# A fused attention and MLP block: a shorter hold in the planned order of the K/V stage, and another order of the first attention tiles

## The chip, the core and the metric

One core of a Trainium2 chip runs the whole block in one launch. The metric is the device time of that launch in microseconds (us), the median over several executions. A second source is one execution taken by the hardware profiler, in which every instruction has a start and a duration. The engines: PE (TensorE, matrix products), DVE (VectorE), ACT (ScalarE), POOL (GpSimd), and SP, whose queue issues nearly all DMAs. Each engine executes its own instructions strictly in the order in which the program lists them; semaphores make one wait for another.

## The reference

```python
def reference(A_x, A_wqkv, A_wo, B_x, B_W_gate, B_W_up, B_W_down):
    x = A_x                                     # (1, 2048, 1024) bf16
    h = x + attention(layernorm(x), A_wqkv, A_wo)
    return h + glu(layernorm(h), B_W_gate, B_W_up, B_W_down)

# attention: 32 heads of 32; phi(t) = where(t > 0, t + 1, exp(t)) + 1e-6
#   q, k, v = split(x @ wqkv);  pq, pk = phi(q), phi(k)
#   kv = pk^T v and z = sum(pk) per head, over all 2048 tokens
#   o = (pq kv) / (pq z + 1e-6);  result o @ wo
# glu: (relu(x @ W_gate) * (x @ W_up)) @ W_down      with 3584 columns
```

This is linear attention: kv and z need all tokens before the first o can be formed.

## The kernel before

**Tiling.** The 2048 tokens are 16 tiles of 128. The big products (K, V, Q, gate, up, down) are done as 2 x 2 block products with seven partial products in place of eight. One such block product is a `Quad` (lines 326 to 368). It works in three PSUM banks, A, D and E: p1 writes A (and ACT's `fork`, line 729, copies A to D), p6 adds into A, of which ACT's `snap` (line 732) takes a copy in SBUF, p5 writes E, p7 adds into A, a second snap follows, p2 adds into D, and after it the results c22 (E plus the second snap) and c11 (D) are read; p4 adds into A (c21), p3 adds into E (c12, with the first snap). So p4 has to wait for the second snap, and p3 for the read of c22. `Quads.run` (line 388) puts p4 and p3 of the previous quad between p1 and p6 of the next. Each p of 4 matmuls of 128x512 lasts some 0.86 us.

The two halves of the 2 x 2 scheme on the token side are tiles t and t + 8, which form pair t. The products need sums of the two halves' transposed, normalised tokens: `left_sums` (line 621) makes four of them on DVE: S1 = a21 + a22, S2 = S1 - a11, S4 = a12 - S2, S3 = a11 - a21. The weights' differences (`WForms.sums`, line 596, and `GW.sums`, line 971) are made on DVE as well.

**Stages.** In this trace: an opening, in which pair 0 runs as plain products; the K/V stage, a K quad and a V quad for each of the pairs 1 to 7, with the accumulation of kv (`kv_acc`, line 809) in banks 5 to 7, to about 122 us; the Q stage for the two blocks s = 0 and s = 1 of 512 columns each; the attention tiles of block 0 (`Tile_`, line 1004), woven into the Q quads of block 1, between 145 and 197 us; the first gate and up products with the attention tiles of block 1 woven in; gate and up to some 566 us; the down products to the end.

**The norm chain of a tile in the K/V stage** (`Norm`, lines 644 to 708). The x tile is loaded (SP). For tiles of the first half (t < 8) DVE takes the statistics (`stat`, two instructions, and `aggr`); for tiles of the second half ACT does, with a copy that sums up and a square that sums up (lines 664 and 667), between which POOL forms the negated mean (`neg`). Two short ACT steps form 1/std (`rstd_`, lines 681 and 683), POOL normalises the tile (`finish`, line 699), and SP issues a transposing DMA (line 701) and the load of a tile two pairs on. After tile 15 the four loads of WQ's parts follow on SP (lines 703 to 707).

**phi** (`phi_quad`, line 743): of each K or Q result ACT takes exp, DVE a clamp (`phi_clamp`) and a join (`phi_join`); c12 and c22 are added on DVE first (line 756), and `exp2` and `join2` treat both together.

**An attention tile** (`Tile_`): `group` for three groups of heads (PE products with kvz into one of banks 5 to 7, two short ACT steps, one DVE multiplication), after which SP transposes o; `wo(0)` and `wo(1)` (8 matmuls each, then a residual add on DVE); `square` (store of h by SP, negated mean), `square2` (ACT), `norm` (two ACT steps, POOL's normalisation, SP's transpose into the buffer that the gate and up products read). A tile with i = 1 also starts `left_sums` some ticks later (lines 1084 to 1086): the one with tt = 1 for two tiles' columns, those with tt = 2 and 3 for one.

**What sets the order.** Nothing is issued directly. `Plan.take` (line 115) records each instruction as a node with its predecessors, an estimated length (`hold`) and latency; so in the profile all instructions stand at line 123. The program text only gives TensorE's nominal order, by which `order` (line 182) gives each node a latest due time (`late`). `schedule` (line 202) then plays the engines forward on its own estimated clock, in nanoseconds, and lists each engine's instructions. TensorE takes the ready node that is earliest in the nominal order, within a window. Every other engine takes, of the nodes that are ready, the one with the earliest due time; but if a node with a due time more than 1500 ns earlier will be ready within `wait`, the engine is left idle until then and takes that one. `wait` is a multiple of the length of the instruction that could run now:

```python
    SHORT = 215000.0                                       # line 43
    wait = (1.2 if s < self.SHORT else 0.5) * v.hold       # line 246
```

The orders that come out are fixed in the program; the chip's own times do not change them.

Of the kernel before, what the change touches and what calls it, by code (L numbers as in the profile page):

```python
# [32 lines left out]
class Plan:  # L33
# [6 lines left out]
    WINDOW = 6000.0  # L40
    AHEAD = 120000.0
    OPENING = 45000.0
    SHORT = 215000.0

    class Node:
        __slots__ = ("eng", "calls", "preds", "hold", "lat", "open", "dma", "late", "ready", "left", "start", "nom")
# [155 lines left out]
    def schedule(self):  # L202
        nodes = self.nodes
        succs = self.order()
        engines = ("tensor", "vector", "scalar", "gpsimd", "sync")
        avail = {e: [] for e in engines}
        clock = {e: 0.0 for e in engines}
        for i, v in enumerate(nodes):
            v.left, v.ready = len(v.preds), max(0.0, v.late - self.AHEAD) if v.dma else 0.0
            if v.eng != "tensor" and v.late > 2.0 * self.OPENING:  # L210

                v.ready = max(v.ready, self.OPENING)
            if not v.left:
                avail[v.eng].append(i)
        pe = [i for i, v in enumerate(nodes) if v.eng == "tensor"]
        done, first, wire, out = set(), 0, 0.0, []
        while True:
            best = None
            for e in engines:
                a = avail[e]  # L220
                if not a:
                    continue
                if e == "sync":
                    for i in a:
                        v = nodes[i]
                        if v.late - max(clock[e], v.ready) > 6000.0:
                            v.ready = max(v.ready, wire - 2000.0)
                if e == "tensor":
                    while first < len(pe) and pe[first] in done:
                        first += 1  # L230
                    limit = nodes[pe[first]].nom + self.WINDOW
                    a = [i for i in a if nodes[i].nom <= limit]
                    if not a:
                        continue
                s = max(clock[e], min(nodes[i].ready for i in a))
                if best is None or s < best[0]:
                    best = (s, e, a)
            if best is None:
                break
            s, e, a = best  # L240
            now = [i for i in a if nodes[i].ready <= s]
            i = min(now, key=lambda i: (nodes[i].nom if e == "tensor" else nodes[i].late, i))
            v = nodes[i]
            if e != "tensor":

                wait = (1.2 if s < self.SHORT else 0.5) * v.hold
                soon = [j for j in a if s < nodes[j].ready < s + wait and nodes[j].late < v.late - 1500.0]
                if soon:
                    i = min(soon, key=lambda j: (nodes[j].late, j))
                    v = nodes[i]  # L250
                    s = v.ready
            v.start = s
            clock[e] = s + v.hold
            end = s + v.hold + v.lat
            if v.dma:
                wire = max(wire, s + v.hold) + v.dma
                end = wire + v.lat - v.dma + min(4000.0, max(0.0, 0.25 * (v.late - s)))
            elif e == "sync":

                end = max(end, min(wire + 800.0, end + 2500.0))  # L260
            avail[e].remove(i)
            done.add(i)
            out.append(i)
            for j in succs[i]:
                w = nodes[j]
                r = clock[e] if w.eng == e else end
                w.ready = max(w.ready, r)
                w.left -= 1
                if not w.left:
                    avail[w.eng].append(j)  # L270
        assert len(out) == len(nodes)
        self.span = max(clock.values())
        return out
# [205 lines left out]
def block_kernel(ctx: ExitStack, tc: tile.TileContext, x, wqkv, wo, wg, wu, wd, out, H: int):  # L479
    nc = tc.nc  # L480
    P = 128
# [12 lines left out]
    SW = 512  # L494
    NS = 2
# [296 lines left out]
    def v_quad(p):  # L792
        v = v_ring()

        def blk(i, j):
            return v[:, i, j * KH:(j + 1) * KH, 0:P]

        def copy(i, j):
            return lambda ps: nc.scalar.copy(out=blk(i, j), in_=split(ps))

        def add(i, j):
            return lambda ps, u: nc.vector.tensor_tensor(out=blk(i, j), in0=split(ps), in1=split(u), op=ALU.add)

        return v, Quad(tok_prod(p, WV), fork, snap,
                       {"c11": copy(0, 0), "c12": add(0, 1), "c21": copy(1, 0), "c22": add(1, 1)}, five_banks)
# [106 lines left out]
    for p in range(1, NP):  # L912
# [6 lines left out]
        v, vq = v_quad(p)  # L919
# [166 lines left out]
                return (lag_s[0], chain_of(*left_sums(self.s * SW + (self.tt + 1 - n) * P, n * P)))  # L1086

    lag_s, turned = [3], []
    tiles = [Tile_(s, i, tt) for s in range(NS) for tt in range(SW // P) for i in range(2)]

    def w(m, j):
        return lambda: tiles[m].wo(j)
# [440 lines left out]
@with_exitstack  # L1533
def kernel(
    ctx: ExitStack,
    tc: tile.TileContext,
    A_x: bass.AP,
    A_wqkv: bass.AP,
    A_wo: bass.AP,
    B_x: bass.AP,  # L1540
    B_W_gate: bass.AP,
    B_W_up: bass.AP,
    B_W_down: bass.AP,
    out: bass.AP,
):
    block_kernel(tc, A_x, A_wqkv, A_wo, B_W_gate, B_W_up, B_W_down, out, H=32)
# [30 lines left out]
```

## Time and profile before

| what | us |
|---|---|
| median of 4 executions | 726.79 (726.66 to 727.04) |
| the profiled execution, its time | 726.7 |
| its span, first to last instruction | 724.9 |
| TensorE not busy within the span | 13.7 |
| ACT busy, DVE busy in 90 to 110 us | 9.7 and 12.3 of 20 |
| ACT busy, DVE busy in 30 to 50 us | 14.6 and 16.8 of 20 |
| ACT busy, DVE busy in 200 to 210 us | 6.9 and 9.6 of 10 |

The page of a profile gives for each engine the busy time, its share of the span and the number of instructions; then the span in 40 slices, a digit each, in tenths of the slice. A timeline lists instructions in order of time, equal ones that follow each other in one line: start, us from that start to the end of the last, engine, line, operation, output and input with partitions x elements and type, count, and in brackets the idle time of the engine just before, with the engine or DMA whose signal ended it. An instruction's duration holds some 0.1 us of its end that overlaps the next on the same engine. Times in the text are us from the start of the span.

### The profile page before, as it was taken

What the parts mean: (1) busy time and instruction counts of PE and PEld (TensorE: products, weight loads), DVE (VectorE), ACT (ScalarE), POOL (GpSimd) and SP (SyncE); (2) the same over time, 40 slices, a digit from 0 to 9 for tenths busy, and PEclk for the clock granted to TensorE, in tenths of its full rate; (3) what the DMA queues carried; (4) which work ended last, traced back from release to release, by engine and by line L of the source; (5) the groups of instructions that cost most, each with busy time, mean ns of one, the idle gap of its engine ahead of it and who ended that gap; (6) DMA issues with size and microseconds to landing.
All of it is one profiled execution on the core that took longest, in us unless ns stands there. A gap on an engine that the chain in (4) does not pass through costs nothing.

```text
span 724.9 us, 11180 instructions
## 1 busy us (share of the span) xinstructions
PE 711.2 (98%) x4112; PEld 396.9 (55%) x4163; DVE 566.4 (78%) x954; ACT 277.1 (38%) x540; POOL 81.8 (11%) x88
## 2 busy tenths in 40 slices
PE   8998999999999999999999999999999999999998
PEld 3444545444444444444444444444444688888887
DVE  6887765788897965566766968769858879899996
ACT  5787644666655343333333333333333220001100
POOL 1343100002201220000000000000000004001452
PEclk9999999999999999999999999999999999999999
DMA  9544805249855540446145584685681878777974
GB/s 287 149 89 101 200 4 183 52 92 212 199 123 146 131 102 1 128 142 182 59 145 181 169 252 144 199 262 184 201 262 51 275 261 213 213 267 234 248 78 60
DMA packets 156503, 117.40 MB, mean 162 GB/s; under 512 B 54944, under 2 KB 140192, under 8 KB 156320
## 3 DMA queue, kind: packets, MB, share of 16 engines
q1 hardware_dynamic: 148832, 113.01, 54.0%
q0 software_dynamic: 7616, 3.67, 4.8%
q8 instruction: 32, 0.52, 0.3%
q14 instruction: 23, 0.19, 0.1%
HBM read 70.52 MB, written 34.08 MB: 144 GB/s over the span
## 4 chain that ended last, share of the span: by engine, by line
PE 88%; ACT 2%; DVE 1%; issue 1%; DMA 0%; POOL 0%; ACTq 0%; DVEq 0%
PE psum L123 88%; ACT mem L123 1%; DVE mem L123 1%; DMA mem<-mem 0%; ACT tiny L123 0%; ACT psum L123 0%; DVE tiny L123 0%; POOL tiny L123 0%; ACTq L123 0%; DVEq L123 0%
## 5 line engine op out<-in xcount | busy, mean ns | idle before, releaser
L123 PE MATMUL psum<-mem 128*128 128x512 bf16 (+4 forms) x4096 | 710.3, 334 | 10.2 <-ACT mem L123 2.5
L123 PEld LDWEIGHTS <-mem 128*128 128x128 f16 (+1 forms) x4163 | 396.9, 98 | 324.2 <-issue 11.0
L123 DVE TENSOR_TENSOR mem<-psum,mem 128x512 f32<-128x512 f32 (+2 forms) x240 | 187.3, 794 | 102.1 <-ACT mem L123 70.8
L123 DVE TENSOR_TENSOR mem<-mem 128x512 f16<-128x512 bf16 (+8 forms) x400 | 244.1, 650 | 8.2 <-DMA mem<-mem 2.9
L123 ACT COPY mem<-psum 128x512 f32<-128x512 f32 (+2 forms) x124 | 92.7, 749 | 215.3 <-PE psum L123 211.1
L123 ACT COPY psum<-psum 128x512 f32<-128x512 f32 (+1 forms) x68 | 49.1, 722 | 158.3 <-PE psum L123 156.1
L123 POOL DMA_DIRECT2D out_dram<-mem x28 | 34.1, 1299 | 412.1 <-DVE mem L123 412.0
L123 POOL TENSOR_SCALAR mem<-mem,tiny 128x1024 bf16<-128x1024 bf16 x28 | 40.7, 1455 | 181.4 <-ACT tiny L123 168.9
L123 ACT ACTIVATE mem<-psum 128x512 bf16<-128x512 f32 x90 | 53.7, 597 | 18.9 <-PE psum L123 18.2
L123 DVE SCALAR_TENSOR_TENSOR mem<-mem 128x512 bf16<-128x512 bf16 (+1 forms) x71 | 57.3, 807 | 1.2
L123 DVE SCALAR_TENSOR_TENSOR mem<-psum,mem 128x512 bf16<-128x512 f32 x66 | 45.2, 687 | 12.5 <-PE psum L123 10.2
L123 DVE TENSOR_SCALAR mem<-mem 128x512 bf16<-128x512 bf16 (+1 forms) x49 | 17.3, 354 | 19.9 <-ACT mem L123 19.1
L123 ACT ACTIVATE mem<-mem,tiny 128x1024 bf16<-128x1024 bf16 x24 | 27.5, 1144 | 8.4 <-DVE tiny L123 5.9
L123 DVE TENSOR_TENSOR mem<-psum,tiny 128x384 bf16<-128x384 f32 (+1 forms) x48 | 22.8, 507 | 4.3 <-ACT tiny L123 3.9
L123 ACT ACTIVATE mem<-mem 128x1024 bf16<-128x1024 f32 (+1 forms) x23 | 24.3, 1056 | 2.9 <-DVE mem L123 2.7
L123 ACT ACTIVATE tiny<-tiny 128x1 f32<-128x1 f32 (+2 forms) x112 | 22.5, 206 | 6.5 <-DVE tiny L123 3.7
L123 ACT ACTIVATE tiny<-psum 128x12 f32<-128x12 f32 (+1 forms) x48 | 8.0, 170 | 17.5 <-PE psum L123 17.2
L123 DVE BATCH_NORM_STATS2 tiny<-mem 128x6 f32<-128x512 bf16 x16 | 10.3, 683 | 2.5 <-DMA mem<-in_A_x_dram 2.5
L123 ACT CAST mem<-psum 128x512 bf16<-128x512 f32 x18 | 10.6, 587 | 4.2 <-PE psum L123 3.7
L123 POOL TENSOR_SCALAR tiny<-tiny 128x1 f32<-128x1 f32 x14 | 5.3, 383 | 39.0 <-ACT mem L123 21.4
L123 ACT ACTIVATION_READ_ACCUMULATOR mem<-mem,tiny 128x1 f32 x24 | 4.5, 188 | 0.0
L123 DVE TENSOR_SCALAR tiny<-tiny 128x1 f32<-128x1 f32 x16 | 3.4, 210 | 0.4
(18 smaller groups left out, 14.4 us busy)
## 6 DMA issues: line engine op xcount, KB each, us to landing
l_dram<-mem SPq DMA_DIRECT2D x98, 128.0 KB, 2.3
mem<-l_dram SPq DMA_DIRECT2D x12, 896.0 KB, 6.3
mem<-in_A_x_dram SPq DMA_DIRECT2D x32, 256.0 KB, 3.0
mem<-in_B_W_up_dram SPq DMA_DIRECT2D x14, 512.0 KB, 5.4
mem<-in_B_W_gate_dram SPq DMA_DIRECT2D x14, 512.0 KB, 4.3
mem<-in_B_W_down_dram SPq DMA_DIRECT2D x28, 256.0 KB, 3.8
r_dram<-mem SPq DMA_DIRECT2D x56, 128.0 KB, 2.0
mem<-r_dram SPq DMA_DIRECT2D x8, 896.0 KB, 5.2
```

The costliest lines, as they stand in the source:

```text
L123: call = lambda: getattr(getattr(self.nc, eng), op)(*args, **k)
```

## The change

The planner's rule gets a lower bound: the long hold (1.2 of an instruction's length) now applies only between 120000 and 215000 ns of the planner's clock, and the short one (0.5) before and after. And the list of attention tiles of block 0 is ordered by half first: tt = 0 to 3 of half 0, then tt = 0 to 3 of half 1, where the halves alternated; block 1 keeps its order.

```diff
-    SHORT = 215000.0
+    MIXED = (120000.0, 215000.0)
...
-                wait = (1.2 if s < self.SHORT else 0.5) * v.hold
+                wait = (1.2 if self.MIXED[0] < s < self.MIXED[1] else 0.5) * v.hold
...
-    tiles = [Tile_(s, i, tt) for s in range(NS) for tt in range(SW // P) for i in range(2)]
+    tiles = [Tile_(0, i, tt) for i in range(2) for tt in range(SW // P)]
+    tiles += [Tile_(1, i, tt) for tt in range(SW // P) for i in range(2)]
```

Compared as lists, both programs hold the same instructions on each engine. The places at which the lists differ, given in the times that the instructions have in the trace of before: SP from 15 to 18 us (tile 2's load ahead of tile 9's transpose), 55 to 85 and 151 to 191; DVE from 17 to 111 and 150 to 227; ACT from 29 to 79 and 149 to 188; POOL from 34 to 189; PE from 149 to 184 (other tiles in the same places) and 209 to 212 (one p5 product of the gate quads ahead of a p3). Everywhere else they are the same.

In the K/V stage, for example, ACT's list around tile 13's square, from the snap at 52.57 us of the trace of before on, reads:

```
before: snap 1; square of tile 13; ln step of 13; exp of c11; exp step of 13; snap 2; fork
after:  square of tile 13; ln step of 13; snap 1; exp step of 13; exp of c11; ln and exp step of tile 6; snap 2; fork
```

## The prediction

> **What bounds the kernel now.** I read the page first (busy times, slices), then the waits of TensorE, then the timelines of TensorE, ScalarE, GpSimd and VectorE around its gaps.
>
> ```profile
> PE 711.2 (98%) x4112; PEld 396.9 (55%) x4163; DVE 566.4 (78%) x954; ACT 277.1 (38%) x540; POOL 81.8 (11%) x88
> PE   8998999999999999999999999999999999999998
> ...
> PEclk9999999999999999999999999999999999999999
> ```
>
> TensorE is busy for 711.2 of 724.9 us at full granted clock, and the change leaves its products as they are. Only the 13.7 us in which it is not busy can move. Of these, windows put 3.7 into the first 30 us, 2.5 into 30 to 70, some 1.9 into 149 to 210 and 3.5 behind 700, where no engine's order changes (the orders of both programs differ only between 15 and 227 us of this trace).
>
> ```profile
> 30.40 25.34 PE L123 MATMUL psum<-mem 128*128 128x512 bf16 x137 [1.42 <-DVE mem L123]
> 57.61 2.75 PE L123 MATMUL psum<-mem 128*128 128x512 f16 x12 [1.87 <-ACT mem L123]
> 152.20 19.52 PE L123 MATMUL psum<-mem 128*128 128x512 bf16 x110 [0.57 <-DMA mem<-mem]
> 172.06 4.95 PE L123 MATMUL psum<-mem 128*128 128x512 bf16 x27 [0.34 <-DVE mem L123]
> 177.35 2.87 PE L123 MATMUL psum<-mem 128*128 128x512 bf16 x14 [0.34 <-DVE mem L123]
> ```
>
> In brackets stands the idle time ahead of the piece. The two gaps that matter are in the K/V stage: 1.42 us (product p3 of pair 1's K quad waits until VectorE has read bank E) and 1.87 us (p4 of pair 3's K quad waits until ScalarE has snapshot bank A). How the second comes about:
>
> ```profile
> 50.50 4.33 POOL L123 TENSOR_SCALAR mem<-mem,tiny 128x1024 bf16<-128x1024 bf16 x2
> 54.80 0.20 POOL L123 TENSOR_SCALAR tiny<-tiny 128x1 f32<-128x1 f32 x1
> ...
> 52.57 0.57 ACT L123 COPY mem<-psum 128x512 f32<-128x512 f32 x1
> 55.04 1.15 ACT L123 ACTIVATE mem<-mem,tiny 128x1024 bf16<-128x1024 bf16 x1 [1.89 <-POOL tiny L123]
> ...
> 56.99 0.58 ACT L123 COPY mem<-psum 128x512 f32<-128x512 f32 x1
> ```
>
> GpSimd normalises tiles 12 and 5 (4.33 us), then forms tile 13's negated mean. ScalarE stands 1.89 us for that mean, squares tile 13 (1.15), and only then makes the snapshot (56.99) that TensorE waits for. The normalisation is not urgent; being late, it has come to lie in front of urgent work.
>
> **The change, part by part.** No instruction is added or removed, on any engine or queue; orders differ.
>
> *Shorter hold before 120 us of planner time.* An engine now waits at most 0.5, not 1.2, of an instruction's length for more urgent work. So in the K/V stage statistics, normalisation and sums move forward past snapshots, forks and phi work; nothing urgent moves forward past them. I followed the new queues by hand with this trace's durations; times below are of this trace, the new ones with a "now".
>
> First gap. VectorE before:
>
> ```profile
> 20.54 3.49 DVE L123 TENSOR_TENSOR mem<-mem 128x512 f16<-128x512 bf16 x5 [2.23 <-DMA mem<-mem]
> ...
> 24.89 4.66 DVE L123 TENSOR_TENSOR mem<-mem 128x2048 f16<-128x2048 bf16 x4
> 29.47 0.28 DVE L123 TENSOR_SCALAR mem<-mem 128x512 bf16<-128x512 bf16 x1
> 29.67 0.68 DVE L123 TENSOR_TENSOR mem<-psum,mem 128x512 f32<-128x512 f32 x1
> ```
>
> The 2.23 us of idleness at 18.3 (tile 9's transpose has to land) is now filled with one weight difference (1.13), a clamp (0.33) and a join (0.61), which leave the queue behind: -2.07. On SP, tile 2's load is now ahead of tile 9's transpose: +0.5. Two statistics of tile 3 (0.60 each) are now ahead of the add at 29.67: +1.2. Net -0.4; the gap goes from 1.42 to about 1.0. Bounds: -1.4 (gap gone), and +1.2 if the filling buys nothing.
>
> Second gap, all in shifted time (0.4 earlier). Tile 12's second 1/std step stood at 50.09, behind two snapshots, a cast and an exp (1.07); now it stands at 45.2, just behind its square and one snapshot. So tile 12's normalisation starts at 45.3, not 50.50; tile 5's follows at 47.8; tile 13's mean is there by 49.7 and its square, behind a cast that ends at 50.2, starts then and not at 55.04. The 1.89 us go. What is late next: the snapshot is now also behind tile 6's two 1/std steps, which wait for VectorE, which waits for tile 12's transpose. 45.3 + 2.5 (GpSimd, half of 4.33 taken upward) + 1.24 (issue) + 2.2 (landing: tile 10's issue ended at 32.00, the sum that needs it began at 34.22) = 51.2. Behind it three left sums (0.34 each), an add (0.60), a left sum, two statistics (1.2) and the aggregate (0.2): 54.6. Two 1/std steps (0.4) and the snapshot (0.58): 55.6. TensorE wants it at 55.37 - 0.4 = 55.0. So about 0.6 of the old gap (2.0 between matmul starts) stays: -1.4. Bounds: -2.0 and 0.
>
> Rest of the stage. I went through every product up to 118 us whose buffer is freed less than 1.6 us before it. The tightest are again adds on VectorE with left sums in front: tile 14's transpose must land first (now at 67.3; the add behind is wanted at 69.4), then tile 15's (now 72.7; wanted 76.5, with 2.4 us of work between: 1.3 to spare). A join that now precedes the c22 add (43, 58, 71, 97, 110 us) falls into idleness of 0.27 to 0.60 ahead of that add: nothing, at most 0.3 each. WQ's loads follow tile 15's transpose and start some 10 us sooner; their sums move with them, into VectorE's idle stretches (82.88: 2.24 us idle). Cost zero.
>
> *First halves' tiles first.* Tile slots on TensorE keep their places, only which tile fills them changes; per slot the same matmuls, three group normalisations, two residual adds, square, normalisation and transpose. Gaps of 0.57, 0.34 and 0.34 stand, since what makes them (the first transpose of o; a gate-weight difference of 1.07 in front of a residual add) stands at the same place. What moves: the left sums need both halves, so those of the first two blocks (four sums, 0.6 to 1.1 us) go from 180-186 to behind 190 us, where VectorE has less room: 8.09 of 10 us busy in 190 to 200, 9.60 in 200 to 210, all of 210 to 220. The new order puts the three S4 sums (0.60 + 2 x 0.34, some 1.3 us) last, at about 207.5 to 209.3, and one p5 product ahead of the p3 that needs them; p3 then starts at 209.7. Gate-weight differences give way (earliest use 221 us). I take 0; bounds -0.4 and +1.3 (all of the S4 work on the path).
>
> Sum: -0.4 - 1.4 + 0 = -1.8. The profiled execution took 726.7 (span 724.9 and 1.8 around it), the median is 726.79: forecast **724.9**.
>
> A rule that speaks against it: normalisations on GpSimd took 4.95 (25.79, two of them) and 4.33 us where an undisturbed one took 1.19 (57.25), and a weight difference 1.98 (27.49) where others took 1.13. The Trainium skill, SBUF — State Buffer, section "SBUF: two separate sides", calls the port pair of VectorE and GpSimd an exclusive lock: whoever comes second stands for the whole instruction, also against a VectorE operation with two SBUF inputs. By that rule each early normalisation can cost VectorE 1.19 us, and with one such on the chain the sum would be -0.6, 726.1; rows say only that it happens in some places (the add on the path reads PSUM and SBUF and kept its 0.67 to 0.69 everywhere).
>
> **Rivals.**
> *The waits only change their name* (0.24): the second gap stays whole, because tile 6's 1/std steps, now in front of the snapshot, come late. For it: the slowest two normalisations (2.5 each) put 12's landing 1.2 us later than the fastest, and everything behind it is one chain. Against: ScalarE's own queue gets to them 4 us sooner. 726.7 - 0.4 + 0 = 726.3. The attention's pile-up (+1.3, so 726.2) counts here too.
> *Left sums in front of the phi work* (slower, 0.17): VectorE is in order, and tile 15's left sum is now three places ahead of the add that frees bank E for p3 of pair 6's V quad. In this trace tile 15's transpose was issued at 80.97 and its sum ran at 84.94. Each us of landing after 74.0 costs TensorE a us. If the chain through SP, ScalarE and GpSimd advances by half of what I worked out (9.8 us, counted on TensorE's clock), it lands at 77.6: +3.6, 728.5. Against: tile 15's square stands, on ScalarE, ahead of work that is needed at 69 us.
> *It doesn't do what it says* (in the first's chance): the order is that of a plan, and the plan's clock is not the chip's.
>
> **How the numbers follow.** My forecast 0.59 (own range 723.8 to 726.0), unchanged name or pile-up 0.24, slower 0.17. A difference of 0.2% (1.45 us) is what a measurement tells from none: faster means below 725.3. Of my own case some 0.07 lie above that. Faster 0.52, same 0.31, slower 0.17. Range: downward -1.4 - 2.0 = -3.4 if both gaps vanish, 723.3; upward to 727.9, toward the slower rival until 2 in 10 are out.
>
> **What would show it.** Right: TensorE's gap ahead of pair 1's p3 near 1.0 us; ScalarE no longer standing for GpSimd before tile 13's square, which runs near 50 us; a gap of at most 0.8 us near 55; TensorE about 1.8 us ahead of its old times from 56 us to the end. Wrong: a gap by VectorE behind a DMA between 64 and 80 us; VectorE without a pause from 190 to 222 us with gaps of TensorE at 201 to 212; the 1.87 us unchanged under another releaser.

## The result, and the profile after

| | us | ratio to before (95%) |
|---|---|---|
| before, median of 52 executions | 726.75 | |
| changed, median of 34 executions | 725.84 (724.48 to 727.14) | 0.9988 (0.9983 to 0.9993) |
| changed, the profiled execution | 725.6, span 723.8 | |

The change gains 0.9 us: clear of noise, since the interval of the ratio ends below 1, but half of the 1.8 us of the forecast and less than the 0.2% (1.45 us) that the prediction calls a difference. The busy line of the page and TensorE's timeline of the changed kernel:

```profile
PE 711.7 (98%) x4112; PEld 396.6 (55%) x4163; DVE 564.5 (78%) x954; ACT 277.3 (38%) x540; POOL 78.6 (11%) x88
```

```profile
29.41 25.69 PE L123 MATMUL psum<-mem 128*128 128x512 bf16 x137 [0.50 <-DVE mem L123]
55.67 21.50 PE L123 MATMUL psum<-mem 128*128 128x512 f16 x118 [0.57 <-ACT mem L123]
77.44 2.75 PE L123 MATMUL psum<-mem 128*128 128x512 bf16 x12 [0.26 <-DVE mem L123]
...
151.06 19.54 PE L123 MATMUL psum<-mem 128*128 128x512 bf16 x110 [0.58 <-DMA mem<-mem]
170.95 4.94 PE L123 MATMUL psum<-mem 128*128 128x512 bf16 x27 [0.35 <-DVE mem L123]
176.25 30.61 PE L123 MATMUL psum<-mem 128*128 128x512 bf16 x149 [0.35 <-DVE mem L123]
```

The first gap fell from 1.42 to 0.50 us of idleness, the second from 1.87 to 0.57, under the same releasers. A piece that starts at 77.44 is new: TensorE waits there for VectorE. The three gaps of the attention stand as they stood (0.58, 0.35, 0.35).

For the account I take the start of the same product in two traces and write the difference (negative: sooner than before). The first 13 us differ from one execution to the next although the order of every engine is the same there, so a stage is read from the difference of two columns:

```
us in the trace of before   13     35     50     60     74     82    205    700
changed                  -0.07  -0.99  -0.64  -1.94  -1.58  -1.16  -1.09  -1.17
```

First gap -0.92, 35 to 50 us +0.35, second gap -1.30, 60 to 74 us +0.36, 74 to 82 us +0.42, attention +0.07, the rest of the program -0.08. From 13 us on that is -1.10. How the second gap came down, from ScalarE's and GpSimd's timelines of the changed kernel:

```profile
50.44 1.15 ACT L123 ACTIVATE mem<-mem,tiny 128x1024 bf16<-128x1024 bf16 x1
...
54.71 0.44 ACT L123 ACTIVATE tiny<-tiny 128x1 f32<-128x1 f32 x2 [0.70 <-DVE tiny L123]
55.06 0.57 ACT L123 COPY mem<-psum 128x512 f32<-128x512 f32 x1
```

```profile
45.56 1.20 POOL L123 TENSOR_SCALAR mem<-mem,tiny 128x1024 bf16<-128x1024 bf16 x1 [3.03 <-issue]
...
47.79 1.99 POOL L123 TENSOR_SCALAR mem<-mem,tiny 128x1024 bf16<-128x1024 bf16 x1 [0.28 <-ACT tiny L123]
49.75 0.37 POOL L123 TENSOR_SCALAR tiny<-tiny 128x1 f32<-128x1 f32 x1
```

GpSimd normalises tiles 12 and 5 from 45.56 on, tile 13's mean is there at 50.1, and ScalarE squares that tile at 50.44 instead of 55.04, without standing for GpSimd. In place of that wait ScalarE stands 0.70 us for VectorE's aggregate of tile 6, whose two 1/std steps are now ahead of the snapshot at 55.06.

And what is new, from VectorE's timeline of the changed kernel:

```profile
67.73 0.43 DVE L123 TENSOR_TENSOR mem<-mem 128x512 f16<-128x512 bf16 x1 [2.46 <-DMA mem<-mem]
...
68.70 0.69 DVE L123 SCALAR_TENSOR_TENSOR mem<-psum,mem 128x512 bf16<-128x512 f32 x1
69.31 0.68 DVE L123 TENSOR_TENSOR mem<-psum,mem 128x512 f32<-128x512 f32 x1
...
74.76 0.43 DVE L123 TENSOR_TENSOR mem<-mem 128x512 f16<-128x512 bf16 x1 [2.15 <-DMA mem<-mem]
...
75.56 1.23 DVE L123 SCALAR_TENSOR_TENSOR mem<-mem 128x1024 bf16<-128x1024 f32 x1
76.70 0.68 DVE L123 TENSOR_TENSOR mem<-psum,mem 128x512 bf16<-128x512 f32 x1
```

At 68.70 a join stands in front of the c22 add (69.31) that frees bank E: TensorE's lead shrinks by 0.23 us between the matmuls of p4 and p3; the same pair at 41.44 and 42.05 costs 0.23 more. At 74.76 VectorE has stood 2.15 us for tile 15's transpose; clamp, join and the V add that frees bank E (76.70) follow in its queue, and p3 of pair 6's V quad starts 0.43 us late. The remaining 0.13 at 41 and at 68 us is a snapshot that ScalarE reaches late behind norm steps.

### The profile page after: what moved, and what is told of

Its sections match the earlier page's. It is cut to its first block, busy times and chain, and to the rows that moved or that the text cites. A ratio compares the mean times of both kernels' runs of the same rounds, so it can differ in the third digit from the quotient of the medians.

```text
span 723.8 us, 11175 instructions
## 1 busy us (share of the span) xinstructions
PE 711.7 (98%) x4112; PEld 396.6 (55%) x4163; DVE 564.5 (78%) x954; ACT 277.3 (38%) x540; POOL 78.6 (11%) x88
## 4 chain that ended last, share of the span: by engine, by line
PE 84%; DVE 2%; ACT 1%; DMA 1%; issue 1%; ACTq 0%; DVEq 0%
PE psum L123 84%; DVE mem L123 2%; DMA mem<-mem 1%; ACT mem L123 1%; ACT tiny L123 0%; ACT psum L123 0%; DVE tiny L123 0%; ACTq L123 0%; DVEq L123 0%
## 5 line engine op out<-in xcount | busy, mean ns | idle before, releaser
L123 POOL TENSOR_SCALAR mem<-mem,tiny 128x1024 bf16<-128x1024 bf16 x28 | 38.4, 1371 | 196.6 <-ACT tiny L123 180.4
```

Of the source, the lines that this page charges most:

```text
L123: call = lambda: getattr(getattr(self.nc, eng), op)(*args, **k)
```

## The experiments

In each, the edit is against the changed kernel unless it says otherwise. "Lead" is TensorE's lead over before, counted from 13 us on as above.

### One part of the change at a time

The hold alone (the old list of tiles), run twice, and the new list of tiles alone (the old hold):

```diff
 hold_only, hold_only2
-    tiles = [Tile_(0, i, tt) for i in range(2) for tt in range(SW // P)]
-    tiles += [Tile_(1, i, tt) for tt in range(SW // P) for i in range(2)]
+    tiles = [Tile_(s, i, tt) for s in range(NS) for tt in range(SW // P) for i in range(2)]
 tiles_only
-                wait = (1.2 if self.MIXED[0] < s < self.MIXED[1] else 0.5) * v.hold
+                wait = (1.2 if s < self.MIXED else 0.5) * v.hold
-    MIXED = (120000.0, 215000.0)
+    MIXED = 215000.0
```

> The changed kernel with the old order of the attention's tiles: only the hold differs from the kernel before. Theory (the hold does everything, the order of tiles is worth nothing): the same as the changed kernel, 0.9 us below before, ratio 0.9988; TensorE 1.1 to 1.2 us ahead from 78 us to the end. Rival (the hold is worth the forecast 1.8 us and the new order of tiles gives half of it back): 1.6 to 1.8 us below before.

> The same kernel as in the first run of this study (the hold alone, old order of tiles), whose profiled execution was no use. Theory: ratio 0.9988 to 0.9992; in the trace the first gap is 0.67 us, the second either 0.74 or 1.62, the gaps after 149 us those of the kernel before. Rival: the new order of tiles is worth a gain of 0.4 us, seen as larger gaps here between 149 and 212 us.

> The kernel before with the new order of the attention's tiles alone. Theory: no difference, 0.0 us within 0.3, TensorE's gaps between 149 and 212 us unchanged (0.57, 0.34, 0.34 of idleness). Rival (left sums pile up on VectorE after 190 us): 0.7 to 0.9 us slower, with a gap of TensorE near 207 us.

| | median, us | before beside it | ratio (95%) |
|---|---|---|---|
| hold_only | 726.34 | 726.77 | 0.9992 (0.9983 to 1.0002) |
| hold_only2 | 726.51 | 726.91 | 0.9991 (0.9982 to 1.0000) |
| tiles_only | 726.96 | 726.77 | 1.0000 (0.9992 to 1.0009) |

```
us in the trace of before   13     35     50     60     74     82    205    700
hold_only2               +0.74  -0.23  +0.11  -1.19  -0.85  -0.50  -0.48  -0.52
tiles_only               -0.50  -0.47  -0.47  -0.42  -0.41  -0.41  -0.34  -0.43
```

The profiled execution of hold_only was an outlier of 2,696 us, and nothing is read from it. In hold_only2 the hold alone leaves every step of the changed kernel: -0.97, +0.34, -1.30, +0.34, +0.35, and nothing behind, a lead of 1.26. The new list of tiles moves TensorE by 0.07 us from 13 us to the end; the gaps behind 149 us are the same in all four traces. The step "first halves' tiles first: 0" holds. The medians put hold_only some 0.4 us above the changed kernel; the intervals overlap, and no place in the traces shows it. That stays open.

### Taking the new gaps away, and the two old ones

to62 ends the short hold at 62 us of the planner's clock in place of 120; `best` also holds for 0.8 us of the planner's clock ahead of the first gap, which puts tile 3's second statistic behind the clamp and the add, and keeps tile 6's first 1/std step (node 319) back until the snapshot has been placed; rstd6 does this last alone.

```diff
 to62
-                wait = (1.2 if self.MIXED[0] < s < self.MIXED[1] else 0.5) * v.hold
+                wait = (1.2 if any(a < s < b for a, b in self.MIXED) else 0.5) * v.hold
-    MIXED = (120000.0, 215000.0)
+    MIXED = ((62000.0, 215000.0),)
 best
+    MIXED = ((26500.0, 27300.0), (62000.0, 215000.0))
+    FLOOR = {319: 54500.0}
...
+            v.ready = max(v.ready, self.FLOOR.get(i, 0.0))
 rstd6
+    MIXED = ((120000.0, 215000.0),)
+    FLOOR = {319: 54500.0}
```

> The changed kernel with the long hold back from 62 us of planner time on instead of 120; on TensorE, ScalarE, GpSimd and SyncE the order is that of the changed kernel, on VectorE it differs only between 67 and 110 us. Theory (the missing gain sits in new waits on VectorE behind a join and behind tile 15's left sum): the gaps of 0.23 us at 69.6 and 0.43 us at 76.8 go, TensorE 1.8 us ahead after 78 us, time 1.5 to 1.8 us below before (ratio 0.9975 to 0.9979). Rival (TensorE, now further ahead, only meets the next late buffer): 0.9 to 1.2 us below before, gaps of the same sum elsewhere between 64 and 100 us.

> The kernel of the run before in this list (long hold from 62 us on) with two more holds: tile 3's second statistic kept behind the clamp and the add ahead of the first gap, tile 6's two 1/std steps kept behind the snapshot at the second gap. Theory (each of the gaps is set by the instruction named in the queue ahead of the reader, and gains add): first gap 0.67 to about 0.1 us, second gap 0.74 to about 0.1, together 2.7 to 3.1 us below before (ratio 0.9957 to 0.9963). Rival (the second gap is set by VectorE's chain from tile 12's transpose, and what TensorE wins earlier it loses there): 1.6 to 2.2 us below before.

> The changed kernel with tile 6's two 1/std steps kept behind the snapshot that the second gap waits for; nothing else is moved on any engine. Theory (what is late next at the second gap is VectorE's aggregate of tile 6, through these two steps, as the prediction had it): the snapshot runs 0.5 to 1.5 us sooner, second gap 0.1 to 0.4 us with whatever left sum, time 0.7 to 1.2 us below the changed kernel's (ratio to before 0.9972 to 0.9979). Rival (the snapshot is late for its own reader's sake, TensorE and VectorE having lost the time elsewhere): within 0.3 us of the changed kernel.

| | median, us | before beside it | ratio (95%) |
|---|---|---|---|
| to62 | 725.59 | 726.77 | 0.9983 (0.9974 to 0.9992) |
| best | 724.83 | 726.77 | 0.9973 (0.9964 to 0.9982) |
| rstd6 | 724.99 | 726.91 | 0.9976 (0.9967 to 0.9985) |

```
us in the trace of before   13     35     50     60     74     82    205    700
to62                     +0.07  -0.84  -0.50  -0.91  -0.79  -0.79  -0.73  -0.82
best                     -0.44  -1.70  -1.37  -2.99  -3.11  -3.11  -3.35  -3.44
rstd6                    +0.06  -0.86  -0.52  -2.15  -2.08  -1.89  -2.15  -2.24
```

In to62 the gaps that the expectation puts at 69.6 and 76.8 us are gone (60 to 82 us: +0.12 in place of +0.78), as the theory had it; the median is 1.2 us below before, less than the 1.5 to 1.8 expected. But the second gap gave only 0.41 us where the changed kernel, with the same order on every engine up to 62 us, got 1.30. TensorE's timeline of to62, then VectorE's and GpSimd's at the place:

```profile
56.70 43.61 PE L123 MATMUL psum<-mem 128*128 128x512 f16 x235 [1.46 <-ACT mem L123]
```

```profile
52.97 1.30 DVE L123 TENSOR_TENSOR mem<-mem 128x512 f16<-128x512 bf16 x1
```

```profile
52.80 1.20 POOL L123 TENSOR_SCALAR mem<-mem,tiny 128x1024 bf16<-128x1024 bf16 x1 [2.54 <-issue]
```

and the same two instructions in the changed kernel:

```profile
52.82 0.42 DVE L123 TENSOR_TENSOR mem<-mem 128x512 f16<-128x512 bf16 x1
```

```profile
52.66 1.49 POOL L123 TENSOR_SCALAR mem<-mem,tiny 128x1024 bf16<-128x1024 bf16 x1 [2.54 <-issue]
```

One of the two stands for the other: either GpSimd's normalisation of tile 13 takes 1.20 and the left sum 1.30, or the left sum takes 0.42 and the normalisation 1.49. The statistics, the aggregate, the 1/std steps and the snapshot are queued behind the left sum, so the first outcome costs TensorE 0.88 us.

In rstd6 the snapshot no longer depends on any of that. ScalarE's timeline, and TensorE's:

```profile
54.40 0.58 ACT L124 COPY mem<-psum 128x512 f32<-128x512 f32 x1 [0.27 <-PE psum L124]
54.88 0.44 ACT L124 ACTIVATE tiny<-tiny 128x1 f32<-128x1 f32 x2
```

```profile
56.33 43.95 PE L124 MATMUL psum<-mem 128*128 128x512 bf16 x232 [0.24 <-DVE mem L124]
```

The snapshot waits for TensorE alone and the second gap is gone at p4; what is late next is one product on, p3 with 0.24 us of idleness behind the c22 add. The second gap now gives 1.63 in place of 1.30 us. Not all of rstd6's lead comes from there: 0.28 us more come at 130 us, where a wait of TensorE for a snapshot, 0.14 us of idleness in the changed kernel, is gone in all three traces that keep tile 6's steps back. No order differs at that place, and no run tells why. `best` has the lead that the theory asked for (3.0 us), but its median shows 1.9.

### The port that VectorE and GpSimd share

no_norm2 is the kernel before without GpSimd's normalisation of tile 2 (node 134); norm13_out is the changed kernel without that of tile 13 (node 274):

```diff
-            for f in self.nodes[i].calls:
+            for f in self.nodes[i].calls if i != 134 else []:
```

> The kernel before with GpSimd's normalisation of tile 2 (2.68 us at 25.8 in its trace) left out; tile 2 enters the products un-normalised, all orders stand. Theory (the third weight difference took 2.06 instead of 1.13 us because GpSimd held the shared port, and this, not the queue alone, made the first gap): the difference at 27.5 takes 1.1 to 1.3 us, the first gap falls from 1.42 to 0.5 to 0.6 us. Rival (the difference is long for another reason, or the other normalisation takes the port at once): unchanged, 1.2 to 1.5 us.

> The changed kernel with GpSimd's normalisation of tile 13 (1.48 us at 52.7 in its trace) left out; tile 13 enters the products un-normalised, all orders and all other instructions stand. Theory (in some executions VectorE's left sum beside it stands 0.9 us for the port the two engines share, as it did in the run with the long hold from 62 us on, 1.30 instead of 0.42 us, and the snapshot at the second gap is late by as much): in the profile the left sum near 53 us takes 0.42 us and the second gap is 0.7 us; the times lie 0.3 to 0.6 us below the changed kernel's (so 1.2 to 1.5 below before, ratio 0.9979 to 0.9983) and are spread less than its 2.7 us. Rival (the long left sum was one odd execution): ratio 0.9988 and the same spread.

no_norm2, VectorE, GpSimd and TensorE ahead of and at the first gap:

```profile
25.49 3.82 DVE L123 TENSOR_TENSOR mem<-mem 128x2048 f16<-128x2048 bf16 x4
```

```profile
29.05 1.45 POOL L123 TENSOR_SCALAR mem<-mem,tiny 128x1024 bf16<-128x1024 bf16 x1 [4.34 <-DVE mem L123]
```

```profile
30.17 25.34 PE L123 MATMUL psum<-mem 128*128 128x512 bf16 x137 [0.52 <-DVE mem L123]
```

The group of four takes 3.82 us where it took 4.66 in before: 0.84 us of the first gap was VectorE standing for GpSimd's first normalisation. With the old order kept, the first gap falls to 0.52 us, close to where the change brought it (0.50). TensorE gains 0.90 us there (from +0.66 at 13 us to -0.24 at 35) and loses 0.1 of it to the end; the second gap (1.91 us of idleness) stands.

norm13_out: median 725.54 against 726.91, ratio 0.9981 (0.9972 to 0.9990), as the theory said (0.9979 to 0.9983); eleven executions lie within 1.6 us, the changed kernel's 34 within 2.7. Its left sum at 52.9 took 0.42 us and its second gap 0.57. By itself this is weak, since the intervals overlap and eleven executions spread less than 34 in any case; a second trace of two kernels decides it:

> The changed kernel once more, for a second trace of it. Theory P: either the left sum near 52.8 us or GpSimd's normalisation beside it is long (1.3 against 0.42, or 1.5 against 1.2), and the second gap is 1.62 or 0.74 us with it. Theory O: the second gap 0.74, TensorE's lead from 13 us on to the end 1.0 to 1.3 us, whatever the opening.

> The same kernel as the run with three holds (its profiled execution was the shortest of ten: TensorE 3.0 us ahead of before from the opening to the end, but its median only 1.9 us below). Question: where the other executions lose the 1 us. Theory P (a stall of VectorE for the port it shares with GpSimd, which comes in some executions and not in others): this trace has one or two instructions with two SBUF inputs that take 0.7 us or more over their usual length, and a gap of TensorE behind them. Theory O (only the opening differs from execution to execution): the gaps from 12 us on are those of the first trace within 0.2 us, and TensorE's lead over before, counted from 13 us on, is 2.8 to 3.1 us again. Median 724.4 to 725.2 under both.

```
us in the trace of before   13     35     50     60     74     82    205    700
after_again              -0.09  -1.05  -0.72  -1.14  -0.79  -0.37  -0.33  -0.42
best_again               -0.21  -1.60  -1.26  -2.00  -2.13  -2.13  -2.37  -2.46
```

VectorE and GpSimd in after_again:

```profile
52.75 1.29 DVE L123 TENSOR_TENSOR mem<-mem 128x512 f16<-128x512 bf16 x1
```

```profile
52.58 1.19 POOL L123 TENSOR_SCALAR mem<-mem,tiny 128x1024 bf16<-128x1024 bf16 x1 [2.54 <-issue]
```

The same program, and the other outcome: the second gap gives 0.42 in place of 1.30, the lead is 0.33 in place of 1.10, and this execution took 726.33. In best_again the left sum took 1.29 as well; the c22 add behind it makes a gap of 1.29 us between matmuls where the first trace had 0.41, and the lead is 2.25 in place of 3.00. Median 724.48 against 726.68, ratio 0.9970 (0.9959 to 0.9982): theory P, not O. Of the nine traces that have this pair of instructions in this order, three show the long left sum (to62, after_again, best_again). A few nanoseconds go with the outcome: in the six with the short left sum it starts 0.164 to 0.165 us behind GpSimd's normalisation, in the three with the long one 0.169 to 0.172. GpSimd's record begins first in all nine, so the records don't show which instruction comes to the port first; that this distance decides is a reading of nine traces, which no run tests.

### Why tile 15's transpose landed late

xr_late puts the attention's first residual loads (`group`, 256 KB each) behind the WQ loads on SP; wq_late issues the WQ loads (512 KB each) later:

```diff
 xr_late
-            v.left, v.ready = len(v.preds), max(0.0, v.late - self.AHEAD) if v.dma else 0.0
+            v.left, v.ready = len(v.preds), max(0.0, v.late - (70000.0 if 140000.0 < v.late < 152000.0 else self.AHEAD)) if v.dma else 0.0
 wq_late: the same with 28000.0 if 104000.0 < v.late < 114000.0
```

> The changed kernel with the attention's first residual loads (256 KB each, issued by SyncE at 66.0 and 68.8, the second just ahead of tile 15's transpose) put behind the WQ loads; no other engine's order changes. Question: why tile 15's transpose took 3.1 to 3.7 us from the end of its issue to the left sum that reads it, where tile 14's took 1.9. Theory A (the load ahead of it in the queues): now 1.9 to 2.3 us, the gap of 0.43 us near 77 us gone. Theory B (the four WQ loads of 512 KB behind it share the wires): still 3.1 to 3.7 us, gap unchanged. Time within 0.6 us of the changed kernel's either way.

> The changed kernel with the four WQ loads issued some 5 us later, after tile 15's transpose has landed; SyncE's order and VectorE's behind 79 us change, nothing ahead of that. Theory A (the residual load ahead of the transpose delays it): from the end of the issue to the left sum still 3.1 to 3.7 us, gap of 0.4 us near 77 us unchanged. Theory B (the WQ loads behind it do): 1.9 to 2.3 us, gap gone. Time within 0.6 us of the changed kernel's either way.

SP's queue in the changed kernel, and VectorE's left sum of tile 15 in xr_late:

```profile
68.76 0.51 SPq L123 DMA_DIRECT2D mem<-in_A_x_dram  x1
70.17 1.24 SPq L123 DMA_TRANSPOSE mem<-mem  x1
71.45 2.92 SPq L123 DMA_DIRECT2D mem<-in_A_wqkv_dram  x4
```

```profile
73.46 0.42 DVE L123 TENSOR_TENSOR mem<-mem 128x512 f16<-128x512 bf16 x1 [1.39 <-DMA mem<-mem]
```

Tile 14's left sum, at 67.73, ran 1.87 us after the end of its transpose's issue (65.86). For tile 15 that is 3.35 us in the changed kernel (71.41 to 74.76), 2.60 without the residual load ahead (70.86 to 73.46), 3.16 in wq_late. In xr_late the gap at 77 us is gone (lead from 60 to 82 us: +0.35 in place of +0.78) and one execution took 724.59. In wq_late a third residual load slipped in right behind the transpose, so it tells nothing of the WQ loads alone; its gap was 0.24 us.

That the load ahead makes the 0.75 us is not shown, because the landing varies as much without it being touched. From the end of the issue of tile 15's transpose to its landing, in the traces that have a residual load ahead and the WQ loads behind:

```
after  after_again  hold_only2  norm13_out  rstd6  best  to62  best_again
3.33   3.32         3.26        3.72        3.11   2.80  2.53  2.47
```

The 2.58 us of xr_late lie inside this range. The WQ loads behind don't do it alone either: in before, tiles_only and no_norm2 the same transpose has them right behind it and landed in 1.86 to 1.87 us. And tile 7's transpose in the changed kernel (67.41), issued 0.92 us behind a residual load, landed in 1.88. Shown: where VectorE's order is the changed one, the gap goes with the landing, from none (2.58) over 0.19 (3.11) to 0.45 us (3.72). What makes the landing long stays open.

## Why the prediction was half right

**First gap: mis-sized.** The prediction took -0.4, measured is -0.92. Its three terms came out: the idleness filled (-2.07), the later start of the left sums (21.15 for 20.54: +0.61 for +0.5) and two statistics (1.28 us, 1.19 to the next start, for 1.2). Together they are -0.27; a pause of 0.12 us between two weight differences and the 0.07 us by which the opening was shorter, which the lead leaves out, bring them to -0.08. VectorE's timeline of the changed kernel:

```profile
21.15 6.22 DVE L123 TENSOR_TENSOR mem<-mem 128x512 f16<-128x512 bf16 x8 [0.62 <-DMA mem<-mem]
27.29 1.28 DVE L123 BATCH_NORM_STATS2 tiny<-mem 128x6 f32<-128x512 bf16 x2
...
28.67 0.69 DVE L123 TENSOR_TENSOR mem<-psum,mem 128x512 f32<-128x512 f32 x1
```

Nearly all of the gain is a fourth term, which is missing: in the new order the differences end at 27.4, and GpSimd, whose normalisation starts at 25.7, gets the port beside the statistics, which do not stand for it (0.69 and 0.68 us, as at 48.04 and 49.23 us of before). That is -0.84, and no_norm2 shows it by itself. The prediction had quoted the long difference (1.98 us), but only as a cost that the new order might bring; on the path it was a cost that the old order had. That the first gap gained more than forecast is luck.

**Second gap: right in size and in its last steps, by luck in its start.** -1.4 was predicted, measured is -1.30; 0.57 us of idleness is left, 0.7 between matmul starts, for the 0.6 of the prediction. The end of the chain was the one worked out (aggregate until 54.6, two 1/std steps, snapshot until 55.6; measured 54.68 and 55.63), and rstd6 shows that it is these steps that hold the rest. The start was not. The prediction let VectorE wait for tile 12's transpose, landing at 51.2 behind a normalisation of 2.5 us. The normalisation took 1.20 us (at 45.56), and the transpose landed at 49.81. SP's queue and VectorE's timeline of the changed kernel:

```profile
46.78 1.72 SPq L123 DMA_TRANSPOSE mem<-mem  x1
```

```profile
48.62 0.68 DVE L123 TENSOR_TENSOR mem<-psum,mem 128x512 bf16<-128x512 f32 x1
49.22 3.08 DVE L123 TENSOR_TENSOR mem<-mem 128x512 f16<-128x512 bf16 x7
52.22 0.69 DVE L123 TENSOR_TENSOR mem<-psum,mem 128x512 bf16<-128x512 f32 x1
```

VectorE did not wait for it: from 41.1 us on it worked without a pause of 0.1 us, and it came to tile 12's first left sum at 51.09, the fifth of this group of seven, behind four left sums of pair 0. Its own earlier work ended where the prediction had put the landing.

**Port lock: right to weigh.** The Trainium skill, SBUF — State Buffer, section "SBUF: two separate sides", says that whichever of such a VectorE and such a GpSimd instruction starts first keeps the pair for all its length; the pairs 1.20/1.30 and 1.49/0.42 us agree in that one of the two is long each time. By that rule the prediction had 726.1 with one stall on the chain; the trace that has the stall at the second gap took 726.33. That the two are close is partly chance, since the stall cost 0.88 us and not 1.19, and other terms were off too. What the prediction did not see is that both outcomes belong to one program, and that the old order held such a stall.

**Rest of the stage, "cost zero": the step that failed.** At 60 us TensorE was 1.87 us ahead, the 1.8 of the forecast, because the first gap's surplus covered what was lost before 50 us (0.35); at 82 us another 0.78 was gone. So the rest of the stage cost 1.13 us in five places: two joins in front of c22 adds (0.23 each, taken as "nothing, at most 0.3"), two snapshots behind norm steps (0.13 each) and tile 15's left sum (0.43). For the last the prediction named the place and the mechanism, as its slower rival and as a sign of being wrong, and gave it 1.3 us to spare. It went by a landing of 2.2 us, that of tile 10's transpose; tile 15's was issued 0.9 us later than worked out and took 3.35 us to land. Why it took so long stays open.

**First halves' tiles first, 0: right** (+0.07 in tiles_only, -0.01 behind 82 us in the changed kernel).

**Sum.** -0.92 - 1.30 + 1.13 gives -1.09, or some -0.3 when GpSimd wins the port; the median lies between, at -0.9. None of the rivals happened as a whole: the slower one did in a small part, and in the trace where GpSimd wins the second gap stays nearly whole (1.45 us of idleness), as the first rival had it, though by the left sum and not by tile 12's landing.

## What to carry to other kernels

When a reorder moves work forward, price each instruction that it puts in front of a bank's reader at its full length, and each DMA on the path with the spread of its landing times (2.5 to 3.7 us here for one transpose), not with one of them. If two instructions that fight for a port start within 0.2 us of each other, look for both outcomes in several traces, and then take readers out from behind the loser: here another place for three short instructions (rstd6) was worth as much again as the whole change (some 0.9 us by the medians), and with two more holds the kernel came to 0.9970 and 0.9973 of the time before. A reader that stays behind the loser keeps its cost, as the c22 add in best_again does.

## What the runs showed that was not expected

- With one fixed program, the left sum and GpSimd's normalisation, starting within 0.2 us of each other, came out in either of two ways: 1.29 to 1.30 us or 0.41 to 0.42 us for the left sum, 3 of 9 traces long, 0.88 us at TensorE. The two starts lay 0.169 to 0.172 us apart in the long cases and 0.164 to 0.165 in the short ones.
- Tile 15's transpose (128x1024 bf16) landed 1.86 to 1.87 us after its issue in three traces with the old order of the K/V stage and 2.47 to 3.72 us after it in ten with the new one. Within the new order the spread is not explained by the loads beside it.
- The first 13 us, in the same order, varied by 1.4 us between traces (-0.67 in xr_late, +0.74 in hold_only2). Whoever compares two traces by their span alone reads this as an effect.
